# First-batch reordering in a fused attention and feed-forward kernel: load order, early scaling, v transposed in the softmax gap, two folds moved ahead, last store split

## The chip, the cores and the metric

The kernel runs on one core of a Trainium2 chip. Times are device microseconds (us) of one launch, the median of several runs. Ratios are the mean time of one kernel's runs over the mean of the other's in the same rounds, so they are not quite the ratio of the medians quoted beside them.

## The reference

```python
# B, N, C = 4, 5824, 256;  q, k, v float32
qn = q / (norm(q, axis=1) + 1e-6)              # norms over the 5824 tokens
kn = k / (norm(k, axis=1) + 1e-6)
s  = kn.transpose(0, 2, 1) @ qn / tau          # 256 x 256 per batch
a  = softmax(s)                                # over the last axis
x  = (v @ a).reshape(B * N, C)
out = (((x @ w1) * (x @ w2)) @ w3) @ w_out     # w1, w2: 256x1024; w3: 1024x1024; w_out: 1024x256
```

## The kernel before

The softmax matrix is folded into w1 and w2 for each batch (eight "folds"), w3 and w_out are multiplied together once (`W_sb`), and then a stream of chunks of 512 tokens runs on the tensor engine: matmuls `a` and `b` on the transposed v (`vT`), a cast of a, a product `abs`, and matmuls `o`. The scores of the next batch are worked in between by a schedule. Only the first batch has nothing to hide behind: its q and k have to be loaded, multiplied (`G`) and squared (`sqq`, `sqk`, the sums for the norms) before anything else. A load runs in pieces of eight tiles of 128 tokens; the last piece has five tiles and a half one.

```python
for nm, pi in [("q", 0), ("k", 2), ("q", 1), ("k", 3), ("q", 2), ("k", 4), ("q", 3)]:
    load_piece(nm, 0, pi)                      # after k0 (two halves) and k1
# ... squares of k ahead by two pieces, products(pi), squares("q", pi), dummies: busy(4)
load_piece("q", 0, 4)
load_piece("k", 0, 5)
load_piece("q", 0, 5, split=True)
# ... weights and v
products(3, whole); squares("q", 3, whole)
products(4, whole); squares("q", 4, whole)
squares("k", 5, range(LAST + 1), end=True)
soft0[0](); busy(2); soft0[1]()                # diagonal of k k^T, its row, the k norms (kr)
squares("q", 5, first); products(5, first)
squares("q", 5, rest, end=True)
soft0[2]()                                     # dq, ss, then r = 1 / norm of q
products(5, rest, end=True)
soft0[3]()                                     # s = G * kr (two halves), e = exp(s * r)
busy(6)
soft0[4]()                                     # row sums, folds 0, 1, 2, transpose of v, fold 3
# folds 4 to 7 come between the first a, b matmuls of the stream
```

The store of the last, small chunk of each batch:

```python
nc.scalar.copy(o[:, 0:2, :], tl[0])            # tl[0]: one PSUM tile [128, 2, 256], float32
nc.sync.dma_start(out=rows[:, NT - 1, :], in_=o[:, 0, :])
nc.sync.dma_start(out=out[b * N + NT * P : (b + 1) * N, :], in_=o[LEFT:, 1, :])
```

And, for later, when the scores of the next batch begin in the schedule (the unit is about 1 us of the tensor engine's time):

```python
loads += [("qk", n, pi, t) for pi, t in enumerate([4.0, 12.0, 27.0, 44.0, 58.0, 72.0])]
t0, t1 = 16.0, 104.0                           # scores from t0 to t1
```

Of the kernel before, what the change touches and what calls it, by code (L numbers as in the profile page):

```python
# [10 lines left out]
AF = mybir.ActivationFunctionType  # L11
ALU = mybir.AluOpType
F32 = DT.float32
# [11 lines left out]
def kernel(  # L25
# [71 lines left out]

    pieces = {}

    def load_piece(nm, n, pi, split=False, part=None):  # L100

        if part == 1:
            t = pieces[nm, n, pi]
            main, _ = qk_main[nm, n]
            g = LAST if pi == NP_ - 1 else PIECE
            lo = PIECE // 2
            nc.gpsimd.dma_start(out=t[:, lo:g, :], in_=main[:, pi * PIECE + lo : pi * PIECE + g, :])
            return
        t = in_pool.tile([P, PIECE, C], BF16, tag=nm, name=f"{nm}_{n}_{pi}", bufs=IN_BUFS[nm])
        main, left = qk_main[nm, n]  # L110
        g = LAST if pi == NP_ - 1 else PIECE
        if pi == NP_ - 1:
            if nm != "v":
                nc.vector.memset(t[LEFT:, g, :], 0.0)
            nc.gpsimd.dma_start(out=t[:LEFT, g, :], in_=left)
        h = PIECE // 2
        cuts = [0, h] if part == 0 else [0, g] if not split else [0, h, g]
        for lo, hi in zip(cuts, cuts[1:]):
            nc.gpsimd.dma_start(out=t[:, lo:hi, :], in_=main[:, pi * PIECE + lo : pi * PIECE + hi, :])  # L119
        pieces[nm, n, pi] = t  # L120

    vTs = {}

# [6 lines left out]
    def pe_transpose(dst, src, tag, on_act):  # L130

        m = psum.tile([P, 8, P], BF16, tag=tag, name=f"tr_{nc.get_next_instruction_name()}", bufs={"ab": 4, "out": 3}[tag])
        for i, blk in enumerate(src):
            nc.tensor.transpose(m[:, i, :], blk, ident_b)
        if on_act is None:
            nc.scalar.copy(dst[:, :4, :], m[:, :4, :])
            nc.vector.tensor_copy(dst[:, 4:, :], m[:, 4:, :])  # L137
        elif on_act:
            nc.scalar.copy(dst, m)
        else:  # L140
            nc.vector.tensor_copy(dst, m)
# [68 lines left out]
    def busy(k):  # L210

        m = psum.tile([P, 512], F32, tag="ab", name=f"warm_{nc.get_next_instruction_name()}", bufs=4)
        for _ in range(k):
            nc.tensor.matmul(m, lhsT=warm[:, :P], rhs=warm, start=True, stop=True, skip_group_check=True)
# [29 lines left out]
    def soft_units(n):  # L244
# [7 lines left out]
        def q_first():  # L252
            d = work.tile([P, CT, P], F32, tag="sq", name="dq", bufs=2)
            nc.vector.tensor_mul(d, S["q"], ident.unsqueeze(1).to_broadcast([P, CT, P]))
            ss = work.tile([P, CT], F32, tag="ss0", name="ss0", bufs=1)
            nc.vector.tensor_reduce(out=ss, in_=d, op=ALU.add, axis=mybir.AxisListType.X)
            q_norm(ss)

        def norms():
            a1 = work.tile([P, 2, C], F32, tag="acc1", name=f"acc1_{n}", bufs=1)  # L260
# [31 lines left out]
                nc.vector.tensor_scalar_mul(r, r, inv_tau)  # L292
            st["r"] = r

        def scaled():
            s = work.tile([P, CT, C], F32, tag="s", name=f"s_{n}", bufs=1)
            for ct in range(CT):
                nc.vector.tensor_mul(s[:, ct, :], G_tiles[n][:, ct, :], st["kr"])
            e = work.tile([P, CT, C], BF16, tag="e", name=f"e_{n}", bufs=2)
            for ct in range(CT):  # L300
                nc.scalar.activation(out=e[:, ct, :], in_=s[:, ct, :], func=AF.Exp, scale=st["r"][:, ct : ct + 1])
            st["e"] = e

        def sum_mm(c2):
            if c2 == 0:
# [15 lines left out]
            sum_mm(0)  # L321
            sum_mm(1)

        def fold_mm(i, c2):
            h, rest = divmod(i, 4)
            w, c1 = divmod(rest, 2)
            if c2 == 0:
                st["fold", i] = psum.tile([P, 512], F32, tag="ab", name=f"fold_{n}_{i}", bufs=4)
            nc.tensor.matmul(  # L329
                st["fold", i], lhsT=st["e"][:, c2, c1 * P : (c1 + 1) * P], rhs=w12[:, c2, w, h * 512 : (h + 1) * 512],  # L330
                start=(c2 == 0), stop=(c2 == CT - 1),
            )
            if c2 == CT - 1:
                dst = Wf[n][:, c1, w, h * 512 : (h + 1) * 512]
                if i % 2 == 0:
                    nc.scalar.activation(out=dst, in_=st["fold", i], func=AF.Copy, scale=st["rs"][:, c1 : c1 + 1])  # L336
                else:
                    nc.vector.tensor_scalar_mul(dst, st["fold", i], st["rs"][:, c1 : c1 + 1])  # L338

        def fold(i):  # L340
            fold_mm(i, 0)
            fold_mm(i, 1)

        def first_folds():
            sum_mm(0)
            fold_mm(0, 0)
            fold_mm(1, 0)
            sum_mm(1)
            fold_mm(0, 1)
            fold_mm(1, 1)  # L350
            fold(2)
            transpose_half_on_pe(0, 0, 0, None)
            fold(3)

        if n == 0:
            return [k_first, k_row, q_first, scaled, first_folds] + [lambda i=i: fold(i) for i in range(4, 8)]
        head = [(0.0, norms), (0.5, k_row), (0.4, q_sums)]
        return head + [(0.0, scaled), (0.2, sums)] + [(0.43, lambda i=i: fold(i)) for i in range(8)]

# [13 lines left out]
    def at(t, cost, fn):  # L373
        seq[0] += 1
        agenda.append((t, seq[0], cost, fn))
# [39 lines left out]
    def emit_out(b, c, j, ab):  # L415
        small = c == NCH - 1
        subs = [0, 64] if small else [0, 128, 256, 384]
        if j == 0:
            out_tiles[b, c] = [
                psum.tile([P, 2, D], F32, tag="out", name=f"o_{b}_{c}_{h}", bufs=3) for h in range(len(subs) // 2)  # L420
            ]
        tl = out_tiles[b, c]
        for s, off in enumerate(subs):
            nc.tensor.matmul(  # L424
                tl[s // 2][:, s % 2, :], lhsT=ab[:, off : off + P], rhs=W_sb[:, j, :],
                start=(j == 0 and s % 2 == 0), stop=(j == FT - 1 and s % 2 == 1), skip_group_check=True,
            )
        clock[0] += len(subs) * (D * MM_COL + MM_FIX)
        if j == FT - 1:
            o = work.tile([P, 4, D], F32, tag="o_sb", name=f"osb_{b}_{c}", bufs=3)  # L430
            rows = out[b * N : b * N + NT * P, :].rearrange("(p i) c -> p i c", i=NT)
            if small:
                nc.scalar.copy(o[:, 0:2, :], tl[0])
                nc.sync.dma_start(out=rows[:, NT - 1, :], in_=o[:, 0, :])
                nc.sync.dma_start(out=out[b * N + NT * P : (b + 1) * N, :], in_=o[LEFT:, 1, :])
            else:
                nc.scalar.copy(o[:, 0:2, :], tl[0])  # L437
                nc.vector.tensor_copy(o[:, 2:4, :], tl[1])  # L438
                nc.sync.dma_start(out=rows[:, 4 * c : 4 * c + 4, :], in_=o)
            del out_tiles[b, c]  # L440
# [5 lines left out]
        load_piece("k", n, pi)  # L446


    busy(14)
    load_piece("k", 0, 0, split=True)  # L450
    load_piece("k", 0, 1)
    masks.make_identity(nc, ident)
    nc.vector.tensor_copy(ident_b, ident)
    w3_wout = vT_pool.tile([P, (NT - 1) * C], BF16, tag="vT", name="w3_wout")
# [11 lines left out]
    w3r = moe_w3.rearrange("(jh jl) l -> jl jh l", jl=P)  # L466
    w1r = moe_w1.rearrange("(ch cl) f -> cl ch f", cl=P)
    w2r = moe_w2.rearrange("(ch cl) f -> cl ch f", cl=P)
    for nm, pi in [("q", 0), ("k", 2), ("q", 1), ("k", 3), ("q", 2), ("k", 4), ("q", 3)]:
        load_piece(nm, 0, pi)  # L470
    soft0 = soft_units(0)
    whole = range(PIECE)
    lo, hi = range(PIECE // 2), range(PIECE // 2, PIECE)
    squares("k", 0, lo)
    busy(2)
    squares("k", 0, hi)
    busy(2)
    squares("k", 1, whole)
    busy(4)
    for pi in range(3):  # L480
        products(pi, whole)
        squares("q", pi, whole)
        squares("k", pi + 2, whole)
        busy(4)
    load_piece("q", 0, 4)
    load_piece("k", 0, 5)
    load_piece("q", 0, 5, split=True)
    for h in range(2):
        hs = slice(h * F // 2, (h + 1) * F // 2)
        nc.gpsimd.dma_start(out=w12[:, :, 0, hs], in_=w1r[:, :, hs])  # L490
        nc.gpsimd.dma_start(out=w12[:, :, 1, hs], in_=w2r[:, :, hs])
        load_piece("v", 0, 0, part=h)
    load_piece("v", 0, 1)
    for h in range(2):
        js = slice(h * FT // 2, (h + 1) * FT // 2)
        nc.gpsimd.dma_start(out=w3_bf[:, js, :], in_=w3r[:, js, :])
    nc.gpsimd.dma_start(out=wout_sb, in_=moe_w_out.rearrange("(lh ll) c -> ll lh c", ll=P))
    load_piece("v", 0, 2)
    products(3, whole)
    squares("q", 3, whole)  # L500
    products(4, whole)
    squares("q", 4, whole)
    squares("k", 5, range(LAST + 1), end=True)
    soft0[0]()
    busy(2)
    soft0[1]()
    first = [LAST] + list(lo)
    rest = range(PIECE // 2, LAST)
    squares("q", 5, first)
    products(5, first)  # L510
    squares("q", 5, rest, end=True)
    soft0[2]()
    products(5, rest, end=True)
    soft0[3]()
    busy(6)
    soft0[4]()
    new_w3T()

# [23 lines left out]
    def make_agenda(b):  # L542
# [1 line left out]
        clock[0] = 0.0  # L544
        n = b + 1
        if b == 0:
            for i in range(4):
                at(0.3 + 0.6 * i, 0.43, soft0[5 + i])
            at(4.0, 0.5, lambda: transpose_half_on_pe(0, 0, 1, False))
            at(7.0, 0.5, lambda: transpose_half_on_pe(0, 1, 0, True))  # L550
            at(8.0, 0.5, lambda: transpose_half_on_pe(0, 1, 1, False))
# [83 lines left out]
```

## Time and profile before

| | before |
|---|---|
| time, median of the first 3 runs | 583.64 us (583.54 to 583.74) |
| span of the profiled run | 581.5 us |
| tensor engine (PE) busy | 569.3 us, 98% |
| vector engine (DVE), scalar engine (ACT) busy | 64%, 59% |
| landing of q piece 3, the last load that the chain waits for | 26.87 us |
| start of the q norms (`dq`) | 36.06 us |
| first matmul of the stream (`a`) | 42.16 us |

The last three rows are from the chain that ended last. How to read it is told in the prediction.

### The profile page before, as it was taken

To read this page: it belongs to the slowest core of one execution; us is meant where nothing else is said; L and a number is where in the kernel's file an instruction comes from. 1 tells how busy PE (TensorE), PEld (TensorE's weight loads), DVE (VectorE), ACT (ScalarE), POOL (GpSimd) and SP (SyncE) were. 2 spreads that over 40 slices of the span, in tenths; PEclk is the share of its full clock that TensorE was granted. 3 is DMA by queue.
4 is the path that set the end of the run, shared out by engine and by line. 5 is a ranking of instruction groups with operands and counts; after the bars stand their busy time and mean duration, and the time that the engine had idled before them with its cause. 6 is when DMAs were issued, how large, how long until landed. Compare 5 with 4: busy or idle time off the path is not lost.

```text
span 581.5 us, 10244 instructions
## 1 busy us (share of the span) xinstructions
PE 569.3 (98%) x3862; PEld 363.1 (62%) x3862; DVE 374.2 (64%) x565; ACT 342.7 (59%) x629; POOL 64.4 (11%) x139
## 2 busy tenths in 40 slices
PE   7989999999999999999999999999999999999996
PEld 4755676766666666666665666666665755666665
DVE  0037645788867567778866667778877556565564
ACT  0037535777765567777765566777765545454454
POOL 4240121111000112002000112001100000000000
PEclk9999999999999999999999999999999999999999
DMA  8999699873442798754564599954554326301011
GB/s 165 212 207 191 115 158 224 171 166 101 113 108 83 144 219 174 133 109 124 114 140 73 126 196 177 166 121 91 145 120 99 84 76 145 87 37 73 38 71 52
DMA packets 65681, 74.85 MB, mean 129 GB/s; under 512 B 45792, under 2 KB 49504, under 8 KB 65632
## 3 DMA queue, kind: packets, MB, share of 16 engines
q0 software_dynamic: 14944, 39.46, 39.9%
q1 hardware_dynamic: 50688, 34.74, 21.4%
q8 instruction: 30, 0.49, 0.3%
q14 instruction: 19, 0.16, 0.1%
HBM read 78.91 MB, written 23.86 MB: 177 GB/s over the span
## 4 chain that ended last, share of the span: by engine, by line
PE 90%; DMA 3%; DVE 2%; ACT 1%; issue 1%; POOL 1%; ACTq 0%; POOLq 0%
PE o L424 27%; PE a L402 26%; PE b L402 26%; PE G L193 5%; DMA q<-in_q_dram 3%; PE fold L329 2%; PE w L530 1%; DVE abs L410 1%; ACT as L408 1%; PE G L238 1%; POOL k L119 1%; PE sqq L226 0%; PE row L268 0%; DVE osb L438 0%; POOL q L119 0%
## 5 line engine op out<-in xcount | busy, mean ns | idle before, releaser
L410 DVE TENSOR_TENSOR abs<-as,b 128x512 bf16<-128x512 bf16 (+1 forms) x384 | 251.9, 658 | 154.9 <-ACT as L408 140.0
L408 ACT CAST as<-a 128x512 bf16<-128x512 f32 (+1 forms) x384 | 215.3, 562 | 173.3 <-PE a L402 86.5
L424 PE MATMUL o<-W_sb,abs 128*128 128x256 bf16 x1472 | 221.5, 273 | 0.2 <-DVE abs L410 0.2
L402 PE MATMUL a<-vT,Wf 128*128 128x512 bf16 x704 | 209.4, 379 | 1.2 <-DVE vT L137 1.0
L402 PEld LDWEIGHTS <-Wf 128*128 128x128 bf16 x1536 | 148.8, 98 | 98.4 <-issue 3.2
L402 PE MATMUL b<-vT,Wf 128*128 128x512 bf16 x704 | 209.4, 379 | 0.1
L424 PEld LDWEIGHTS <-abs 128*128 128x128 bf16 x1472 | 143.4, 98 | 86.7 <-DVE abs L410 0.4
L202 DVE TENSOR_TENSOR acc<-acc,sq 128x1024 f32<-128x1024 f32 x66 | 80.4, 1219 | 0.1
L394 POOL COPY gate_t<-abs 1x1 bf16<-1x1 bf16 x39 | 12.4, 318 | 393.2 <-DVE abs L410 376.8
L193 PE MATMUL G<-k,q 128*128 128x256 bf16 x276 | 50.2, 273 | 0.0
L190 ACT ACTIVATE sq<-q 128x512 f32<-128x512 bf16 x66 | 41.8, 633 | 0.0
L190 ACT ACTIVATE sq<-k 128x512 f32<-128x512 bf16 x66 | 41.6, 631 | 0.0
L438 DVE COPY osb<-o 128x512 f32<-128x512 f32 x44 | 30.1, 685 | 0.4 <-PE o L424 0.4
L193 PEld LDWEIGHTS <-q 128*128 128x128 bf16 x276 | 27.0, 98 | 3.1
L437 ACT COPY osb<-o 128x512 f32<-128x512 f32 x44 | 25.7, 585 | 3.8 <-PE o L424 1.7
L270 ACT ACTIVATE kr<-row 128x256 f32<-128x256 f32 x4 | 1.5, 383 | 34.9 <-PE row L268 34.9
L329 PE MATMUL fold<-w,e 128*128 128x512 bf16 x64 | 16.6, 378 | 0.0
L336 ACT ACTIVATE Wf<-fold,rs 128x512 bf16<-128x512 f32 x16 | 10.9, 687 | 8.5 <-PE fold L329 6.3
L119 POOL DMA_DIRECT2D q<-in_q_dram x25 | 13.5, 540 | 11.1 <-DMA k<-in_k_dram 5.0
L119 POOL DMA_DIRECT2D v<-in_v_dram x24 | 12.9, 537 | 11.7 <-DMA vT<-v 4.6
L119 POOL DMA_DIRECT2D k<-in_k_dram x25 | 13.8, 552 | 2.8 <-DMA k<-in_k_dram 2.0
L338 DVE TENSOR_SCALAR Wf<-fold,rs 128x512 bf16<-128x512 f32 x16 | 11.7, 747 | 1.6 <-PE fold L329 1.5
(101 smaller groups left out, 178.8 us busy)
## 6 DMA issues: line engine op xcount, KB each, us to landing
out_dram<-osb SPq DMA_DIRECT2D x44, 512.0 KB, 3.0
q<-in_q_dram POOLq DMA_DIRECT2D x20, 512.0 KB, 7.0
k<-in_k_dram POOLq DMA_DIRECT2D x19, 512.0 KB, 9.4
v<-in_v_dram POOLq DMA_DIRECT2D x19, 512.0 KB, 5.2
w_wout<-in_moe_w_dram POOLq DMA_DIRECT2D x2, 1024.0 KB, 16.6
k<-in_k_dram POOLq DMA_DIRECT2D x4, 320.0 KB, 6.3
v<-in_v_dram POOLq DMA_DIRECT2D x4, 320.0 KB, 4.9
w<-in_moe_w_dram POOLq DMA_DIRECT2D x4, 256.0 KB, 8.1
```

Source lines behind the costliest of these rows:

```text
L119: nc.gpsimd.dma_start(out=t[:, lo:hi, :], in_=main[:, pi * PIECE + lo : pi * PIECE + hi, :])
L190: nc.scalar.activation(out=dst[:, :, part, :], in_=src[:, o : o + 2, :], func=AF.Square)
L193: nc.tensor.matmul(G[:, ct, :], lhsT=qt[:, i, ct * P : (ct + 1) * P], rhs=kt[:, i, :], start=(pr == 0 and part == 0 and ct == 0), stop=(pr ...
L202: nc.vector.tensor_add(accs[n], accs[n], sqs[0])
L329: nc.tensor.matmul(st["fold", i], lhsT=st["e"][:, c2, c1 * P : (c1 + 1) * P], rhs=w12[:, c2, w, h * 512 : (h + 1) * 512], start=(c2 == 0), ...
L394: nc.gpsimd.tensor_copy(gate_t, last_ab[0][:1, :1])
L402: nc.tensor.matmul(t[:, :n], lhsT=Wf[b][:, ct, w, j * P : (j + 1) * P], rhs=rhs_of(b, c, ct), start=(ct == 0), stop=(ct == CT - 1),)
L408: nc.scalar.copy(a_sb[:, :n], tiles[0][:, :n])
L410: nc.vector.tensor_mul(ab[:, :n], a_sb[:, :n], tiles[1][:, :n])
L424: nc.tensor.matmul(tl[s // 2][:, s % 2, :], lhsT=ab[:, off : off + P], rhs=W_sb[:, j, :], start=(j == 0 and s % 2 == 0), stop=(j == FT - 1 ...
L437: nc.scalar.copy(o[:, 0:2, :], tl[0])
L438: nc.vector.tensor_copy(o[:, 2:4, :], tl[1])
```

## The change

The intent is to shorten the first 42 us: all of k loaded before the last two pieces of q, so that only q's work is left behind the last landing; the last q piece loaded in parts of two tiles; the first scaling of G ahead of the reciprocal of the q norms; the first half of v transposed while the softmax runs on other engines; two more folds before the stream. At the end, the last copy is split over two engines and the last stores over two queues.

```diff
-    load_piece("k", 0, 0, split=True)
-    load_piece("k", 0, 1)
+    load_piece("k", 0, 0, (half,))
+    load_piece("q", 0, 0, (half,))
 ...
-    for nm, pi in [("q", 0), ("k", 2), ("q", 1), ("k", 3), ("q", 2), ("k", 4), ("q", 3)]:
-        load_piece(nm, 0, pi)
+    for pi in range(1, 4):
+        load_piece("k", 0, pi)
+        load_piece("q", 0, pi)
+    load_piece("k", 0, 4)
+    load_piece("k", 0, 5)
 ... (squares and products follow the landings; busy(4) after each round is gone)
     load_piece("q", 0, 4)
-    load_piece("k", 0, 5)
-    load_piece("q", 0, 5, split=True)
+    load_piece("q", 0, 5, (2, 4))
 ...
+        def scaled_first():
+            scale(0)
+            q_norm(st["ss"])
+            scale(1)
+            exps()
 ...
+    parts = [[LAST, 0, 1], [2, 3], [4]]
+    for sl in parts:
+        squares("q", 5, sl, end=sl is parts[-1])
+        if sl is parts[-1]:
+            soft0[2]()
+        products(5, sl, end=sl is parts[-1])
     soft0[3]()
-    busy(6)
+    busy(4)
+    transpose_half_on_pe(0, 0, 0, False)
     soft0[4]()
 ... (in first_folds)
             fold(2)
-            transpose_half_on_pe(0, 0, 0, None)
             fold(3)
+            fold(4, "out")
+            fold(5, "out")
 ... (last chunk of every batch)
-                nc.scalar.copy(o[:, 0:2, :], tl[0])
-                nc.sync.dma_start(out=rows[:, NT - 1, :], in_=o[:, 0, :])
+                nc.scalar.copy(o[:, 0, :], tl[0][:, 0, :])
+                nc.vector.tensor_copy(o[LEFT:, 1, :], tl[0][LEFT:, 1, :])
+                (nc.scalar if b == B - 1 else nc.sync).dma_start(out=rows[:, NT - 1, :], in_=o[:, 0, :])
```

## The prediction

> **What bounds the kernel now.** I read the page's slices first: which engine is full, and when.
>
> ```profile
> PE   7989999999999999999999999999999999999996
> DMA  8999699873442798754564599954554326301011
> GB/s 165 212 207 191 115 158 224 171 166 101 113 108 83 144 219 174 133 109 124 114 140 73 126 196 177 166 121 91 145 120 99 84 76 145 87 37 73 38 71 52
> ```
>
> A slice is 14.5 us. From the third slice on the tensor engine is at 90% or more until the last, so anything this change gains must come from the first 45 us or the last 5; whatever shift arises at the start is carried by a full tensor engine to the end. In the first slices the DMA engines are full too, at about 212 GB/s. Next the chain that ended last, in order of time (start, length, what):
>
> ```profile
> 6.66 20.21 DMA q<-in_q_dram
> 26.87 0.05 issue
> 26.92 1.92 PE G L238 x16
> ...
> 35.91 0.12 PE sqq L226 x2
> 36.04 0.02 issue
> 36.06 0.43 DVE dq L254
> 36.52 0.43 DVE ss L256
> ...
> 37.81 0.33 DVE s L298
> 38.14 0.02 issue
> 38.17 0.52 ACT e L301
> ...
> 39.91 1.26 ACT Wf L336 x2
> 41.17 0.48 ACT vT L136
> 41.66 0.02 issue
> 41.68 0.43 DVE vT L137
> 42.12 0.04 issue
> 42.16 0.59 PE a L402 x2
> ```
>
> Three stretches. Up to 26.87 the loads of q and k bind; from there to 36.04 the tensor engine works without a gap although data still arrives; from 36.06 to 42.16 a serial chain of small vector and scalar operations binds (q norms, scaling, exponential, eviction of the folded weights, copy of the first transposed v), and the tensor engine mostly waits. Third, the timeline of the engine that issues the loads. Apart from the first ten, an issue waits for the load eight places before it, so the end of a wait dates a landing:
>
> ```profile
> 24.70 0.70 POOL L490 DMA_DIRECT2D w<-in_moe_w_dram  x1 [1.89 <-DMA k<-in_k_dram]
> 27.16 0.71 POOL L491 DMA_DIRECT2D w<-in_moe_w_dram  x1 [1.76 <-DMA q<-in_q_dram]
> 29.68 0.54 POOL L119 DMA_DIRECT2D v<-in_v_dram  x1 [1.80 <-DMA q<-in_q_dram]
> 33.09 0.54 POOL L119 DMA_DIRECT2D v<-in_v_dram  x1 [0.49 <-DMA q<-in_q_dram]
> 37.06 0.55 POOL L119 DMA_DIRECT2D v<-in_v_dram  x1 [0.41 <-DMA v<-in_v_dram]
> ```
>
> Counted off, these are the landings of k piece 4, q piece 3, q piece 4, the first half of q piece 5, and the first half of v piece 0. In bytes written (a full piece is 0.524 MB) these are the points 4.19 MB at 24.7, 4.72 at 27.0, 5.24 at 29.6, 5.90 at 33.0 and 6.75 at 37.0 us: all of q and k is 5.96 MB and lands at about 33.4. Last, the end of the timeline:
>
> ```profile
> 577.28 0.59 ACT L433 COPY osb<-o 128x512 f32<-128x512 f32 x1 [0.88 <-PE o L424]
> 577.89 0.33 SPq L434 DMA_DIRECT2D out_dram<-osb  x1
> 578.27 0.49 SPq L435 DMA_DIRECT2D out_dram<-osb  x1
> ```
>
> One copy, then two stores issued one behind the other from the same queue.
>
> **What the Trainium skill says.** "TensorE: Matmul & The Clock Gate", Back-to-back issue gap, gives N/2.4 + 2.5 ns for a warm matmul. The trace agrees: 16 products of 256 columns take 1.75 us in the chain (109 ns each), 16 squares of 128 columns 0.89 us (56 ns each). The same page, Part 1, says that an idle window of about 3.4 us halves the clock. No run so far shows that here; the granted clock is 1.00 even from 6.00 to 9.41 us, where the tensor engine was busy 1.75 of 3.41 us. "DMA: Bandwidth & Descriptors", Anatomy of one DMA, puts about 2 us of fixed time on each transfer, mostly the write receipt; the two last stores, of 128 and 64 KB, took 1.7 and 2.0 us from issue to landing, which agrees. Its section Issuing engines are not separate DMA queues says that issuing from a second engine saves only sequencer time; here that is the 0.38 us between the two last store issues.
>
> **The change, part by part.**
>
> *Load order.* The bytes are the same, so the last q still lands at about 33.4. What changes is what is left to do at each landing. k piece 5 now ends at 5.08 MB and lands at about 29.0 (interpolated), q piece 4 at 5.60 MB, about 31.2. Squares of k, the column sums and the four scalar operations of the k norm (1.8 us, from 34.30 to 36.12 before) leave the tail. What is left after q piece 4: its squares 0.89, its products 1.75, then for the six slots of piece 5 twelve squares at 56 ns (0.67) and twelve products at 109 ns (1.31). The q squares are finished before the last two products, so they end 4.4 us after the landing, at 35.6. With the 0.2 us that the result takes to drain (from 35.75 plus two issues to 36.06 before) the vector engine starts on the q norms at 35.8 against 36.06: gain 0.25. This is the disappointment in the change: before, the squares and the row of k were in the tail, but q piece 4 came 1.6 us sooner, and the two nearly cancel. The two-tile pieces of q land at about 32.2, 33.0 and 33.4, each before the tensor engine comes to it (33.8, 34.8, 35.5), so finer pieces hide nothing more.
>
> *Removed dummy matmuls.* Groups of four dropped after each round were in slack; they cost no time on the path and give none back.
>
> *Scaling ahead of the q norms.* Before, both scalings (0.73 us for two) followed the reciprocal, and the exponential started after the first. Now the first scaling runs while the scalar engine does its logarithm and exponential (36.97 to 37.42), so the exponential starts right after the reciprocal: one scaling less on the path, 0.33 us. The second, 0.4 us, fits beside the first exponential (0.45 us, half of 0.91). From dq at 35.8: reciprocal done at 37.55, exponentials end at 38.5 against 39.1. Gain so far 0.25 + 0.33, about 0.6.
>
> *v transposed in the gap.* Its eight transposes need v's first half, at 37.0 as before (same bytes ahead of it), and take 0.45 us plus drain. One copy on the vector engine, which took 0.68 us at the same shape later on, runs from about 37.9 to 38.6, while the exponentials run. The row sums can then be inverted at 38.85 against 39.46 and the evictions of the folds start at 39.25 against 39.91. Two per engine then take 1.26 us (scalar) and about 1.45 us (vector), and nothing comes between: folds 0 and 1 are out at 40.0, folds 2 and 3 at 40.7. Before, two half copies of v in a row (scalar, then vector) put the first "a" at 42.16. Now the first "a" can start at 40.05 and its "b" at 40.75: with the "a" of 0.43 us the stream is as good as started at 40.3. Gain there 1.85, of which 0.6 was counted above.
>
> *Two folds more ahead of the stream.* Folds 4 and 5 run while the tensor engine would wait for evictions. Four matmuls at 0.216 us: 0.87 us less in the full stream. Their weights (second half of w1) land at 7.01 MB, about 38.2, before they are wanted at 39.5. Their evictions delay the first casts of the stream to about 41.2; the third "a", the first that needs a freed buffer, is due at 42.0, so that just holds. I take 0.2 us off for it.
>
> *Last store.* The copy of 128x512 in 0.59 us becomes two side by side of half the width, about 0.38 us (128x256 from the same memory took that in the k norm), and the stores no longer queue: 0.2 + 0.38, some 0.55 us. The vector engine's extra half copy in the other batches lies beside a full tensor engine.
>
> Sum: 1.85 + 0.87 - 0.2 + 0.55 = 3.1 us. From 583.64 that gives 580.6.
>
> **The rivals.**
>
> *The first v half becomes the wait.* The transposes now stand ahead of the row sums on the in-order tensor engine. If v lands at 38 instead of 37, sums and folds wait for it, and the vector copy then delays the inverse of the sums. For: only 0.3 us lie between my landing plus transposes and the first exponential's end. Against: the same bytes precede it. Each further 1 us costs about 1 us: the time would be 581.5.
>
> *The clock drops.* With k and q landing alternately and dummies gone, the tensor engine has, by my landings, some 0.9 us of work between 11.0 and 14.7 us. For: the skill's idle window. Against: no gap is over 2 us, and a half clock there makes the engine fill up and recover by 20 us, with slack of a quarter until 28. If it dropped in the tail, 4.4 us of work would cost up to 4 more: 584.5.
>
> *Off by the landing of q piece 4.* It leads the new chain; if small transfers slow the queue by 3%, it lands up to 1 us later and the gain of the load order turns into a loss: 581.6. For: more, smaller loads. Against: the DMA engines' share is full and 1 KB rows were already in it.
>
> *The gain is given back.* Later weights (w3, w_out) don't come sooner, so transposes of them could wait. w3's first half should land near 49 us by bytes, and its first use moves from 54.8 to about 52: no wait. I give this little weight; the time would be 582.5 at worst.
>
> **Range and chances.** The central sum is 580.6. The named losses are mostly one-sided, so I put the prediction at 580.8. The upper end takes one of the 1 us rivals plus some of another: 582.2. The lower end takes the chain at its best, with no loss in the stream and q piece 4 half a microsecond sooner: 579.8. A difference of 2% is 11.7 us; no sum here comes near it, as the whole chain from the last landing to the first "a" is under 9 us. Chances: faster 0.01, same 0.97, slower 0.02.
>
> **What would show it.** In the changed profile: the chain leaves the DMA of q near 31.2 instead of 26.87 and has products of q piece 4 behind it; dq near 35.8; the copy of vT on the vector engine over before the inverse of the sums; the first "a" near 40.1; the last landing of loads unchanged. A first "a" later than 41, a wait of the transposes for v, a granted clock below 1.00 in the first 30 us, or a tail in which the tensor engine waits for the last q pieces would prove the matching step wrong. If "a" comes at 40.1 and the time falls by less than 2.5 us, the stream gave it back.

## The result, and the profile after

| | before | after |
|---|---|---|
| time, median | 583.6 us (583.54 to 583.74, 4 runs) | 582.44 us (581.33, 582.36, 582.53, 582.58) |
| ratio | | 0.9976, 95% interval 0.9958 to 0.9993 |
| span of the profiled run | 581.5 us | 579.2 us (the run of 581.33) |
| `dq` starts | 36.06 | 35.77 |
| first `a` (timeline) | 42.16 | 40.82 |
| a fixed place early in the second batch (a gate copy) | 192.26 | 190.02 |
| end of the last matmul | 577.25 | 575.07 |

So the change gains 1.2 us at the median, not 2.8. The one profiled run gained 2.3 us; the three others about 1.1. There are two questions: why the good run gained 2.3 and not 3.1, and what the other three lost.

The slices of the page of the changed kernel (40 slices, busy share in tenths; PEclk is the granted clock):

```profile
PE   8899999999999999999999999999999999999997
PEclk9899999999999999999999999999999999999999
```

The tensor engine's line differs from the one of before in its first three digits and its last. What is new is in the clock's line, which was 9 throughout before: the granted clock falls in the second slice, 14.5 to 29 us. The chain that ended last, in order of time (start, length, what):

```profile
14.34 16.76 DMA q<-in_q_dram
31.11 0.05 issue
31.16 1.07 PE sqq L221 x16
...
35.74 0.02 issue
35.77 0.43 DVE dq L249
...
37.53 0.02 issue
37.56 0.52 ACT e L304
...
38.80 2.18 PE fold L341 x10
40.98 0.43 PE a L415 x2
```

The chain now leaves the loads at the landing of q piece 4, at 31.1, and the tensor engine has 4.6 us of work behind it. From the exponential on it is no longer the evictions that lead to the first `a`, but ten fold matmuls in a row on the tensor engine. The chain counts the first `a` from the end of the folds; its own start, used in the tables, is in the timeline:

```profile
40.82 0.59 PE L415 MATMUL a<-vT,Wf 128*128 128x512 bf16 x2
```

The timeline of the engine that issues the loads, whose waits date the landings of q piece 4 and of the first half of v piece 0, as before:

```profile
31.39 0.70 POOL L506 DMA_DIRECT2D w<-in_moe_w_dram  x1 [1.91 <-DMA q<-in_q_dram]
37.06 0.56 POOL L109 DMA_DIRECT2D v<-in_v_dram  x1 [0.33 <-DMA v<-in_v_dram]
```

Two landmarks for what follows. A tiny copy (the gate of a load) stands at a fixed place in the second batch's program, 13th of its kind; its start tells what the first batch cost. The line of before, then of after:

```profile
192.26 0.18 POOL L394 COPY gate_t<-abs 1x1 bf16<-1x1 bf16 x1 [25.13 <-DVE abs L410]
```

```profile
190.02 0.18 POOL L407 COPY gate_t<-abs 1x1 bf16<-1x1 bf16 x1 [23.45 <-DVE abs L423]
```

From `dq` to this gate is 156.20 us before and 154.25 after. In the experiments this distance repeats to 0.01 us wherever the part between is unaltered (`q4_halves` is the one exception, 154.37), although `dq` itself moves by some tenths from run to run. It is the measure used for single parts below.

The end of the timeline, after:

```profile
575.09 0.37 ACT L446 COPY osb<-o 128x256 f32<-128x256 f32 x1 [0.88 <-PE o L437]
575.49 0.37 ACTq L448 DMA_DIRECT2D out_dram<-osb  x1
575.49 0.43 DVE L447 COPY osb<-o 64x256 f32<-64x256 f32 x1 [0.89 <-ACT osb L446]
575.95 0.49 SPq L449 DMA_DIRECT2D out_dram<-osb  x1
```

The vector engine's half of the copy starts when the scalar engine's ends: the two do not run side by side.

### The profile page after: what moved, and what is told of

Same layout as the page of the kernel before. It is cut to its first block, busy times and chain, and to the rows that moved or that the text cites. A ratio compares the mean times of both kernels' runs of the same rounds, so it can differ in the third digit from the quotient of the medians.

```text
span 579.2 us, 10219 instructions
## 1 busy us (share of the span) xinstructions
PE 567.8 (98%) x3844; PEld 362.9 (63%) x3844; DVE 376.0 (65%) x569; ACT 341.8 (59%) x628; POOL 64.3 (11%) x141
## 4 chain that ended last, share of the span: by engine, by line
PE 90%; DMA 5%; DVE 2%; ACT 1%; issue 1%; POOL 1%; ACTq 0%; POOLq 0%
PE o L437 27%; PE a L415 26%; PE b L415 26%; PE G L188 5%; DMA q<-in_q_dram 5%; PE fold L341 2%; PE w L547 1%; ACT as L421 1%; DVE abs L423 1%; PE G L233 0%; PE sqq L221 0%; POOL k L109 0%; DVE osb L452 0%; ACT e L304 0%; PE row L269 0%
## 5 line engine op out<-in xcount | busy, mean ns | idle before, releaser
L407 POOL COPY gate_t<-abs 1x1 bf16<-1x1 bf16 x39 | 11.2, 287 | 395.9 <-DVE abs L423 379.5
L109 POOL DMA_DIRECT2D q<-in_q_dram x27 | 14.5, 538 | 12.8 <-DMA q<-in_q_dram 6.4
```

The lines of the kernel that those rows point to most:

```text
L109: nc.gpsimd.dma_start(out=pieces[nm, n, pi][:, lo:hi, :], in_=qk_main[nm, n][0][:, pi * PIECE + lo : pi * PIECE + hi, :])
```

## The experiments

There were twelve further runs, two of them of the unaltered changed kernel and two of one version. Each is the changed kernel with one edit, unless said otherwise; all gave the correct result. "Distance" is from `dq` to the gate copy.

### again: the changed kernel unaltered, and warm: the dummies back

```diff
         squares("k", pi, whole)
+        busy(4)                      # warm only; pi = 1, 2, 3
         squares("q", pi, whole)
```

> The changed kernel unaltered, to see how its runs spread: three of its first four took 582.4 to 582.6 us at a mean granted clock of 0.998 to 0.999, one took 581.3 at 0.995. Both theories expect two groups again, about 1.2 us apart. The profile may fall in the slower group; theory A (the clock drops at a place where it is on the path) then expects slices at half clock after 24 us, in the tail of the q loads or the folds, and the first a at about 42 instead of 40.8. Theory B (something other than the clock, such as a later landing of q piece 4 or a stall after 45 us) expects the first a at 40.8 or a late q landing with a full clock in the tail.

> The changed kernel with four dummy matmuls again after the squares of k pieces 1, 2 and 3, in the wait for q. Theory A (the removed dummies let the clock drop, and in most runs that costs time on the path) expects a granted clock of 1.000 in every run, one group only, at about 581.3 us. Theory B (the clock is not what separates the groups) expects a full clock and still two groups, median about 582.4.

Measured: `again` 581.17, 581.34, 581.65, 582.41, 583.07; `warm` 581.31, 582.34, 582.43, 582.72, 582.73. Two groups in both. The half clock is real. In the first changed run it shows in the stretch from 20.38 to 23.79 us (PE, PEld, DVE, ACT and POOL busy, granted clock, DMA share, GB/s):

```profile
20.38:23.79 3.41, 3.41 (x24) 2.67 (x22) 0.00 (x0) 0.00 (x0) 0.85 (x2) 0.50 1.06 211
```

It follows a stretch of the same length in which the tensor engine was busy 1.31 us. But the engine has caught up by 30.8 us and waits 0.40 us for q piece 4. `warm` has a full clock over that stretch, and four of its five runs are still slow. Theory A falls. (The mean clock of a run, 0.998 to 1.000 in `warm`, decides nothing: it also counts a fall after the last matmul, 0.67 over 575 to 580 us in the first changed run, 0.94 in `again`.) The profile of `warm` fell in the slow group and shows the loss elsewhere (timeline of the tensor engine):

```profile
339.23 0.38 PE L188 MATMUL G<-k,q 128*128 128x256 bf16 x2 [0.67 <-DMA k<-in_k_dram]
```

This is the first score matmul for the last batch. It waits for k piece 0, which landed 10.7 us after its issue at 328.53. (The 13.6 and 9.7 us that a later expectation gives for this piece are medians over two loads; the piece's own times are 10.7 in `warm` and 9.3 in `again`.) Across this place, from one gate to the next, `again` takes 8.18 us and `warm` 9.00. In `warm` the first batch also ended 0.45 us later, as its q piece 4 came at 31.47 and not 31.02. Together that is the 1.2 us between the two profiles. The whole run confirms it: from `dq` to the start of the vector engine's last copy, the profiles of the first changed run, `again` and `again_2` take 539.72, 539.73 and 539.72 us, `warm` 540.56. So the spread within the fast group is the drift of `dq`, and 0.84 us come from this one place.

In the kernel before the same matmul started 9.88 us after the issue of k and did not wait:

```profile
340.27 0.38 PE L193 MATMUL G<-k,q 128*128 128x256 bf16 x2
```

There k piece 0 had landed after 9.1 us. The margin was 0.8 us, in `again` 0.6: the place was near an edge already.

### late_scores: the scores of batches 2 and 3 begin later

```diff
-            t0, t1 = 16.0, 104.0
+            t0, t1 = 19.0, 104.0
```

> The changed kernel with the scores of batches 2 and 3 begun 3 us later in their schedule. In the slow run whose trace is at hand, the scores wait 0.67 us for k piece 0 of the last batch, which landed 13.6 us after its issue instead of 9.7. If that wait is what makes the slow group, the group vanishes: all runs 581.0 to 581.8 us. If it is one of several, or the spread comes from the first 45 us, the spread stays, some runs above 582.2.

Measured: 581.52, 581.53, 581.60, 581.78, 581.82. The slow group is gone. Ratio to before 0.9966 (0.9953 to 0.9978). In the same rounds `v_between`, described below and with the scores at their old place, fell into the slow group in its profile too, with the same matmul waiting 0.68 us for the same load, which also took 10.7 us:

```profile
339.94 0.38 PE L191 MATMUL G<-k,q 128*128 128x256 bf16 x2 [0.68 <-DMA k<-in_k_dram]
```

In `order_before`, further down, the load took 9.9 us and the matmul started 0.1 us later than its usual 9.87 us after the issue, just on the edge.

### store_before: the old last store, twice, and again_2: its control

```diff
-                nc.scalar.copy(o[:, 0, :], tl[0][:, 0, :])
-                nc.vector.tensor_copy(o[LEFT:, 1, :], tl[0][LEFT:, 1, :])
-                (nc.scalar if b == B - 1 else nc.sync).dma_start(...)
+                nc.scalar.copy(o[:, 0:2, :], tl[0])
+                nc.sync.dma_start(...)
```

> The changed kernel with the old last store (one copy by the scalar engine, both stores on the one queue) in every batch. Prediction: 0.55 us slower at the end. Trace theory: the two copies of the split run one after the other, so that the split is worth 0.14 us: from the end of the last matmul to the end of the span 4.25 us as before instead of 4.13. On the slow group, two theories: if the split store of the third batch delays the loads behind it (its second store is issued 0.74 us after the first instead of 0.39), the slow group vanishes and all runs lie at 581.3 to 581.8; if k piece 0 of the last batch is merely due on the edge, some runs above 582.2 remain.

> The changed kernel unaltered, as a control on the same chip as the next run. So far 9 of its runs lie between 581.17 and 583.07 us, 5 of them above 582.2. Both theories: again some of these runs above 582.2. If none is, the slow group depends on the chip and the next run decides nothing.

> The changed kernel with the old last store in every batch, again, on the same chip as the control. If the split store of batch 2 (its second store issued 0.74 us after the first instead of 0.40) is what pushes k piece 0 of the last batch over the edge, no run above 582.0. If the edge alone does it, as many slow runs as the control has. At the end of the span, 4.26 us from the last matmul as in the first such run, against 4.1 for the control: 0.1 to 0.15 us slower between the fast groups.

Measured: `store_before` 581.37, 581.40, 581.40, 581.48, 581.84. On another chip, in shared rounds, `again_2` gave 581.49, 582.47, 582.52, 582.69, 582.72 and `store_before_2` 581.40 to 581.66. None of ten runs with the old store is slow, against four of five in the control and nine of all 14 runs of the changed kernel. So the split of the last store makes the slow group, and the traces of `warm` and `v_between` put the loss at the scores for the last batch, not at the end of the last batch, where the split was meant to help. (The edit undoes the extra copy and the new order of stores together; no run parts them.) The store before that place is the one at the end of the second batch; one of the expectations calls it the third batch's. The schedule of its queue, in `again_2`:

```profile
324.57 0.33 SPq L448 DMA_DIRECT2D out_dram<-osb  x1
325.32 0.50 SPq L449 DMA_DIRECT2D out_dram<-osb  x1
```

and in `store_before_2`:

```profile
324.90 0.33 SPq L447 DMA_DIRECT2D out_dram<-osb  x1
325.29 0.50 SPq L448 DMA_DIRECT2D out_dram<-osb  x1
```

With the split the first small store goes out 0.09 us after the v load that was issued at 324.48, without it 0.31 us after one at 324.59, and the gap between the two stores grows from 0.39 to 0.75 us. The first store then lands after 1.8 us with the split, after 5.7 and 5.5 without. Behind the stores come the loads of q and k and the transpose of v that ended late in the slow profiles. But every profile with the split shows the same store times against the v load, to 0.02 us, the fast `again` (k landed after 9.3 us) like the slow `warm` (10.7), and k took 9.5 and 8.7 us in the two profiles with the old store. So the split makes the late landing possible; what makes it happen in one run and not in another is not settled, as the profiles show the late landing and not what blocked it.

At the very end, from the end of the last matmul to the end of the span, the old store takes 4.26 us in `store_before` and 4.25 in the kernel before; the split takes 4.13 in the changed kernel. The split is worth 0.13 us there, not 0.55.

### order_before: the old order of loads and first matmuls

The edit puts back the load sequence, the matmul order and the dummies shown under "The kernel before", with `scaled_first`, the v transpose, the folds and the split store as changed.

```diff
-    for pi in range(1, 4):
-        load_piece("k", 0, pi)
-        load_piece("q", 0, pi)
-    load_piece("k", 0, 4)
-    load_piece("k", 0, 5)
+    for nm, pi in [("q", 0), ("k", 2), ("q", 1), ("k", 3), ("q", 2), ("k", 4), ("q", 3)]:
+        load_piece(nm, 0, pi)
 ... (first loads, squares, products and busy(4) as before)
-    load_piece("q", 0, 5, (2, 4))
+    load_piece("k", 0, 5)
+    load_piece("q", 0, 5, (half,))
```

> The changed kernel with the old order of the first loads and of the matmuls on them (k piece 5 last but one, q piece 5 in two loads, the dummies back); norms, v, folds and store stay as changed. The prediction has the load order at 0.25 us: dq should start near 36.06 instead of 35.77, the first a about 0.3 us later than the 40.82 of the changed kernel. Rival: the landing of q piece 4 drifts by up to half a us between runs, so that the order is worth nothing and dq comes anywhere from 35.6 to 36.1. The clock stays 1.00.

Measured: 581.85 us median (581.79 to 582.24). `dq` at 36.23; with the old order in the kernel before it was 36.06. With the new order the ten profiles (the two versions meant to beat both left out) have it between 35.63 and 36.36, five of them at 36.04 to 36.08. The rival holds: what the order gains is less than the run to run drift of the landing of q piece 4. In the same rounds, on the same chip, three profiles with the new order have `dq` at 36.04 to 36.12, so 0.1 to 0.2 us sooner, from one profile with the old. The distance was 154.25, so nothing else hung on it.

### scale_late, v_between, folds_stream: one part each undone

```diff
 # scale_late
-            scale(0)
             q_norm(st["ss"])
+            scale(0)
             scale(1)
 # v_between: the transpose between folds 2 and 3, copied in two halves
             fold(2)
+            transpose_half_on_pe(0, 0, 0, None)
             fold(3)
-    transpose_half_on_pe(0, 0, 0, False)     # ahead of the sums
 # folds_stream: folds 4 and 5 between the first a, b matmuls again
-            fold(4, "out")
-            fold(5, "out")
```

> The changed kernel with both scalings after the reciprocal again. The prediction: 0.33 us on the path, so the exponential starts 2.1 us after dq instead of 1.8, and the gate near 190 us comes 154.6 us after dq instead of the 154.25 that all runs with the changed chain show. Rival: the row sums and evictions wait for the copy of v (which stands behind the second scaling on the vector engine) and for the second exponential, so that the 0.33 us grows or shrinks there: 154.25 to 154.9.

> The changed kernel with the first v half transposed between folds 2 and 3 again and copied in two halves by the scalar and the vector engine. The prediction gives this part about 1.2 us beside the earlier norms, a first a at 42. Trace theory: the halves run one after the other, as they did before (the second ended its wait on the first), and the copy stands behind evictions; first a at about 41.6 to 42.0, so 0.8 to 1.2 us later than 40.8 measured from dq, of which nothing is regained since the tensor engine waits.

> The changed kernel with folds 4 and 5 back between the first matmuls of the stream. The prediction counted them as 0.87 less 0.2, so 0.67 us slower. Trace theory: the two folds fill a hole that the evictions of folds 0 to 3 leave only in part; without them the first a starts at about 40.1 instead of 40.8, its b waits until 40.8, and the stream, four matmuls of 0.216 us longer, ends about 0.26 us later in all. So the first a 0.7 us after exponentials and sums as before, and the gates of the later batches 0.2 to 0.4 us later (relative to the start of dq) rather than 0.67.

| | distance, us | against 154.25 | first `a` after `dq` | runs, us |
|---|---|---|---|---|
| scale_late | 154.56 | +0.31 | 5.37 | 582.43 (one look) |
| v_between | 154.99 | +0.74 | 5.77 | 581.97, 582.27, 582.96, 583.67 |
| folds_stream | 154.64 | +0.39 | 4.27 | 581.57, 581.64, 581.90, 582.78 |
| changed kernel | 154.25 | | 5.05 | |

The scaling is worth what was predicted. In `v_between` the second half copy shows what it waits for (timeline of the vector engine):

```profile
41.34 0.42 DVE L135 COPY vT<-tr_I-503_504 128x512 bf16<-128x512 bf16 x1 [1.01 <-ACT vT L134]
```

The two halves of one PSUM tile, on two engines, run one after the other, as they did in the kernel before. In `folds_stream` the first `a` comes 0.78 us sooner, but its `b` then waits for folds 2 and 3, and the four fold matmuls are still to be done; the two moved folds are worth 0.39, not 0.67. The three single losses sum to 1.44 us, of the 1.95 that the distance gained in all; the remaining 0.51 is split by no run here: it may be what they are worth together only, or come from the smaller edits beside them, such as the four dummy matmuls for six.

### q4_halves and q4_banks: versions meant to beat both

```diff
 # q4_halves, on top of late_scores
-    load_piece("q", 0, 4)
+    load_piece("q", 0, 4, (half,))
 ... (the first half of v is loaded ahead of the first half of w2)
-    squares("q", 4, whole)
-    products(4, whole)
+    for sl in (lo, hi):
+        squares("q", 4, sl)
+        products(4, sl)
 # q4_banks, on top of that: in the last batch's last chunk
+            if small and b == B - 1:
+                out_tiles[b, c].append(psum.tile([P, CT, C], F32, tag="G", name="o_last", bufs=1))
```

> A version meant to beat both: the later scores, and q piece 4 loaded and worked on in two halves, with the first v half ahead of the second weight of the first fold group. If the tensor engine's work behind the landing of q piece 4 bounds the tail, its first half (0.262 MB, 1.2 us sooner) takes 1.3 us of the work out of the tail: dq near 35.1 to 35.4 instead of 35.6 to 36.1, v lands near 35.9, first a about 0.7 us sooner; 580.9 with all runs within 0.4 us. Rival: the row of k norms now stands where the first half would run, or v and w2 land too late for the earlier sums: less than 0.2 us gained, 581.5.

> The same with the last two output groups in two PSUM tiles, so that their copies do not share one. If the sharing of one PSUM tile is what makes the vector engine's copy wait for the scalar engine's, the two now overlap and the last store is issued about 0.4 us sooner: from the end of the last matmul to the end of the span 3.7 us instead of 4.1; 580.5. Rival: the copies write one tile in the fast memory, and that is what orders them; then they stay serial and nothing changes.

Measured in shared rounds: `q4_halves` 581.15 to 581.39, median 581.26, ratio to before 0.9962; `q4_banks` 580.54 to 580.96, median 580.67, ratio 0.9953 (0.9939 to 0.9967). `dq` came at 35.50, short of the 35.1 to 35.4 hoped for, and 35.24, within it; both are sooner than in any profile of the changed kernel. In `q4_banks` the two copies overlap (end of the timeline):

```profile
574.45 0.37 ACT L450 COPY osb<-o 128x256 f32<-128x256 f32 x1 [0.76 <-PE o L440]
574.56 0.43 DVE L451 COPY osb<-o_last 64x256 f32<-64x256 f32 x1 [0.49 <-PE o_last L440]
574.85 1.18 ACTq L452 DMA_DIRECT2D out_dram<-osb  x1
```

The destination tile is still shared, so it was the shared PSUM tile that ordered the copies (the second tile also lies in another bank, and no run parts tile from bank). That is what the Trainium skill would have told: "PSUM — Partial Sum Buffer", PSUM bank collisions raise a hardware error, says that two engines on one bank in the same partitions collide, reads against reads included, and that a compiler therefore puts a dependency between them. A tile of 2 x 256 float32 values is one such bank. The rest of the hoped-for gain was lost to the issue on the scalar engine's queue: 1.18 us here and 1.20 in `q4_halves`, against 0.37 in the changed kernel, so that from the end of the last matmul to the end of the span took 4.26 us and 4.58, where 3.7 had been expected of `q4_banks`. In `late_scores` the issue took 1.07 us too, so in all three versions with later scores the split store on the scalar engine's queue no longer gains its 0.13 us. `q4_banks` is faster than both kernels: its slowest run is below the fastest of the 14 runs of the changed one, if not in shared rounds with it.

## Why the prediction was right or wrong

The forecast of "within 2%" held. The expected 580.8 us and its range did not hold for the median: 582.44 lies 0.24 us above the upper end, and only the fast group, 581.17 to 581.65, is inside.

**The start of the new chain was right, with some luck.** q piece 4 was put at 31.2 and came at 31.1; `dq` was put at 35.8 and came at 35.77; v's first half was put at 37.0 and came at 37.06, by the end of an issue's wait, which is about 0.2 us after the tensor engine first uses the load (36.83). By that same measure q piece 4 came at 31.39, and the prediction's own points (5.24 MB at 29.6, 5.90 at 33.0) put 5.60 MB at 31.45, not 31.2. The profiled run was also an early one: the ten profiles with the new order have `dq` at 36.04 in the middle, so the predicted gain of 0.25 us is nearer 0.1. That the load order would gain next to nothing, because q piece 4 comes later as k piece 5 leaves the tail, was right too, and `order_before` confirms it. So was the remark that the tensor engine, not the last two-tile loads, bounds the tail: taking half of q piece 4 ahead in `q4_halves` moved `dq`.

**The scaling was right**: 0.33 predicted, 0.31 measured.

**The step "the stream is as good as started at 40.3" failed.** It credited the folds as time won in the stream and, at the same time, let the first `a` start at 40.05, as if folds 4 and 5 stood nowhere. They stand ahead of it in the program, and the trace has them ahead of it on the tensor engine: the first `a` came at 40.82. Evictions would have let it start near 40.0, as `folds_stream` shows (4.27 us after `dq`, so 35.77 + 4.27). The terms of the sum 1.85 + 0.87 - 0.2 = 2.52 us should have been 1.34 (42.16 less 40.82) + 0.87 = 2.21. The gates put it at 2.24 (192.26 less 190.02).

**The step "two side by side" failed.** The last store was put at 0.55 us and measured 0.13. The evidence was in the lines that the prediction itself quotes: the two half copies of v, scalar 41.17 and vector 41.68, out of one PSUM tile, were in a row, and the prediction even says so. It did not carry this over to the two halves of the output tile.

These two account for the profiled run: 2.2 + 0.1 = 2.3 us, as measured, in place of 3.1. (The 2.2 holds the early landing of that run.)

**The step "lies beside a full tensor engine" failed**, and it cost the most. The prediction wrote off the split store in the other batches as hidden. The extra copy is hidden (from `dq` to the end of the last matmul the changed kernel and `store_before_2` both take 539.30 us), but the store moved against the loads behind it, and in 9 of 14 runs the times lie in a group about 1.2 us slower. The wait of 0.7 us for k piece 0, 0.8 us from gate to gate, was seen in both slow profiles of versions with the split and the old start of the scores (`warm`, `v_between`); undoing the split (0 of 10 slow) or giving the scores more time (0 of 5, and 0 of 10 in the two versions built on it) removes the group. The rest of the 1.2 us in `warm` was a later landing at the start; for the other slow runs, which have no profile here, the rest stays open.

**The rival of the clock was right as a mechanism, and right that the slack would take it up.** In eight of the 14 profiles the granted clock fell to 0.50 for about 3.4 us: in `v_between` from 14.3 to 17.8 us, at the end of the thin stretch of 11.0 to 14.7 that the prediction named, in the other seven at about 20 to 24 us, at the end of the next one. The skill's page "TensorE: Matmul & The Clock Gate" (Part 1) has a window of about 3.4 us; the trace shows 3.41 us at 0.50. In the profiled run the engine had caught up before q piece 4 landed, so it cost nothing on the path; in `again_2` only 0.16 us of waiting were left.

**The other rivals.** The late landing of q piece 4 did occur: in eight of the ten profiles with the new order the tensor engine starts on it between 31.35 and 31.74, up to 0.6 us later than in the profiled run, and it is 0.45 us of the loss in `warm`. The transposes waited for v for 0.24 us in `store_before` and 0.18 in `again_2`, with no effect on the distance. That the gain is given back by later weights did not occur: between 40 and 75 us no wait for a load shows in the changed profile.

## What to carry to other kernels

A tail that a change shortens has to be recomputed in program order: what is moved ahead of the first useful instruction delays it, and cannot be counted as both free and gained. When two engines share the eviction of one PSUM tile, look whether their copies overlap: here they did not, at three places, and did once each had its own tile. When a change moves a store by a few tenths of a microsecond, look in the trace for loads that land just before they are needed anywhere after it: a margin of 0.6 us was too small here, starting the consumer 3 units later cured it, and runs in two groups were the sign of it.

## What the Trainium skill lacked or had wrong

- "TensorE: Matmul & The Clock Gate" advises against gaps over about 3 us. Here the clock halved with no gap over 2.10 us, after a stretch of 3.41 us in which the tensor engine was busy 1.31 us; in all eight profiles with a drop, the 3.41 us before it had 1.06 to 1.45 us busy. No threshold follows: `late_scores` has a stretch of 3.41 us with 1.05 us busy (16.6 to 20.0) and no drop, and where the windows lie in a profile without a drop is not known. The page has no figure for the busy share that keeps the clock.
- "DMA: Bandwidth & Descriptors" (Issuing engines are not separate DMA queues) says that issuing from a second engine saves sequencer time, "usually small". For the one store that the scalar engine issued, the issue took 0.37 or 0.38 us in eight profiles and 1.07, 1.18 and 1.20 us in three; the three are the versions with later scores. The page has no such spread; its cause is open.
- No page tells how far a small store among loads can move their landing: k piece 0 landed 9.1 us after its issue in the kernel before, 9.3 in `again` and 10.7 in the two slow profiles, and 9 of 14 runs are slow when two stores of 128 KB and 64 KB, some 4 us before that issue, go out 0.75 us apart, none of ten when they go out 0.39 apart. What decides within the first case is open.
- "PSUM — Partial Sum Buffer" had the dependency between two engines on one bank right, but gives no price for it; here it is the wait of 0.4 us of the second copy.
